# Rows of attention reordered by dimension and head, and another order of attention's steps: gated attention and GLU on one core

## The chip, the cores and the metric

The kernel runs on one core of one Trainium2 chip. The metric is the device time of one execution in microseconds (us). The core has five engines that run their own instruction streams side by side and wait for each other by semaphores: TensorE (PE, matrix products), VectorE (DVE), ScalarE (ACT), GpSimd (POOL) and SyncE (SP). DMAs are issued here from SP's queue, a few from ACT's, and an instruction stream is in order: what stands behind a waiting instruction waits too.

## The reference, cut to what matters

The input is x of 2048 rows by 576. One half is linear attention with 32 heads of 18 dimensions, the other a gated MLP of width 4608, and a gate g per row mixes them.

```python
qkv = (x @ wqkv) as (3, H=32, S, Dh=18); q, k, v = qkv
phi = lambda t: where(t > 0, t + 1, exp(t)) + 1e-6
pq, pk = phi(q), phi(k)
kv = einsum("bhsd,bhse->bhde", pk, v);  z = sum over s of pk
o  = einsum(pq, kv) / (einsum(pq, z) + 1e-6)
a  = o.reshape(S, D) @ wo
b  = (gelu(x @ w_gate) * (x @ w_up)) @ w_down
g  = sigmoid((x * gate_w).sum(-1))
out = g * a + (1 - g) * b
```

## The kernel before, in words

All products are done on TensorE as several products of rounded high and low parts, so that float32 precision is kept. The MLP is a block algorithm with seven products in place of eight. The work has four stages. The first (to about 119 us) projects the keys and sums key features against x. The second (to about 146 us) forms the states `st`, `st4` (keys by values for each head) and the key sums, and begins the queries. The third, which this study is about, runs from 146 to 290 us: a list written out by hand, `PLAN` (lines 33 to 44), of 249 steps. Line 888 calls them in this order, and each step appends its instructions to the engines' streams; so the list sets the order on every engine, and an instruction runs when its operands, its buffer and the ones ahead of it on its engine let it. The fourth stage is the MLP: loops over chains of seven products (line 985) and the down projection (line 1062).

The queries come in four blocks b of 512 rows; blocks 2 and 3 come first in the list, then 0 and 1. Their features are laid over partitions in five groups g of 128, 128, 128, 128 and 64 rows (`QORDER`, line 21, gives the feature at each row). The steps, with the line of their instructions in the profile:

- q(b, g) (L467): PE, 14 products into one of three PSUM buffers `bank` (10 for g = 4). qe (L480, L481): relu and exp on ACT; qd (L485): max and add on DVE, which frees the bank. qs (L475, L476) folds the two halves of group 4, qz (L471) clears.
- so (L595 to L605) takes the states out of PSUM, multiplies them by a mask of "same head" and splits them into high and low parts. ks(g) (L611, L612) forms `zmk`, the key sums of each head as columns, on DVE.
- wl(g) loads wo (SP), ws(g) splits it (L588 ACT, L589 POOL), ho(g) multiplies it with the state (L622 PE), he(g) takes that out (L82 ACT, L83 DVE) to `kw`. ro(g) copies two rows of group 4 into group g by DMA (SP), rd (L634, L635) duplicates group 4.
- h(b, g) splits the query features (L645 ACT, L646 DVE) into one of two `hl` buffers; n(b, g) (L655 PE) multiplies them with `zmk` into `den`, the denominators.
- rc(b, half) takes `den` out (L686 ACT, L687 DVE), forms the reciprocal (L688 DVE) and stores it to DRAM (L689 SP). rl(b, half) (L694 SP) loads it back so that each partition has the reciprocal of its own head, in two DMAs: 126 rows read with the 7 heads outermost and each repeated 18 times, and 2 rows.
- sc(b, t) (L701 DVE) multiplies 128 rows by the reciprocals, sp(b, t) (L706 ACT, L707 and L708 DVE) splits them into one of two `p` buffers, m(b, t) (L717 PE) is 28 products with `kw` into one of two `pair` buffers, mo(b, t) (L724 ACT) scales them by the gate into one of two `ga` buffers and stores that to DRAM from ACT's queue (L726).
- For the MLP: tl, ts, tp load, sum (L313 to L316 DVE) and split (L668 ACT, L671 POOL) blocks of x; al, as, ao and ul, us, uo do sums ahead on POOL with loads and stores; xo(i) stores blocks of x to DRAM (L740 SP); w0 (ACT's queue) and w1 (SP's queue) (L767) load prepared weights; g (L743) loads ACT's table for gelu; f0 to f3 (L790 PE) are the first four of the seven products of the MLP's first chain; o0 to o2 close and open memory pools.

The order of tiles in a buffer ring follows the list: a new tile takes the buffer that the list has freed for the longest time.

Of the kernel before, what the change touches and what calls it, by code (L numbers as in the profile page):

```python
# [15 lines left out]
H, DH = 32, 18  # L16
# [13 lines left out]

PLAN = """
h20 wl4 q24 so q31 al3 h21 ws4 wl0 wl3 qs2 qe24 qz3 ks0 ks2 qe31 wl1 ao1 q30 qd24 ks3 ho4 qd31 ks1 n20 q32 ws0
ws1 qe30 he4 h22 as2 qe32 qd30 n21 ho1 h23 al4 ks4 wl2 ho0 he1 q33 ao2 ro1 n22 ws2 ws3 he0 h24 q34 qe33 qd33 ho2
al5 qs3 ho3 n23 he2 as4 ro2 he3 qd32 n24 qe34 o0 ro0 as3 xo0 rc20 ao4 h30 ro3 qd34 rl20 h31 rc21 qz0 as5 xo1 q00
rl21 q01 qe00 tl0 q02 n30 qe02 qd02 n31 ao3 qd00 h32 qe01 ao5 q03 n32 sc21 ul0 xo2 h33 ul1 sc20 qd01 us0 h34 q04
qe03 ul2 n33 sp20 n34 rd h00 sp21 rc30 us1 qs0 m20 sc22 m21 rc31 qd03 qe04 sp22 sc23 q11 us2 ts0 q10 tl1 rl30
h01 mo21 sp23 tp0 mo20 qz1 qd04 qe10 qe11 n00 rl31 qd11 n01 uo0 m22 h02 qd10 mo22 sc30 m23 sc31 sp30 q12 sp31
mo23 qe12 ts1 uo1 q13 n02 h03 h04 uo2 sc32 m30 tl2 n03 n04 tp1 qd12 rc00 q14 rc01 m31 h10 sc33 n10 h11 sp32 qe13  # L40
mo31 sp33 rl00 qs1 o1 mo30 qd13 n11 h12 qe14 rl01 h13 qd14 m32 mo32 w0 n12 sc00 m33 g sc01 sp00 h14 n13 sp01 n14
mo33 m00 rc10 sc03 sc02 mo00 ts2 sp02 rl10 tp2 rc11 m01 rl11 m02 sp03 o2 sc10 w1 f0 mo02 mo01 f1 m03 sc11 sp10
mo03 sp11 sc12 f2 sc13 m10 sp12 mo10 f3 m11 m12 sp13 mo11 m13 mo12 mo13
"""

SEQUENCE = (1, 6, 2, 7, 5, 4, 3)
# [6 lines left out]
def tile_gated_mix(ctx, tc, xt, xs, xn, wk, wv, wq, wo, wgu, wdn, cst, out):  # L53
    nc = tc.nc
# [15 lines left out]
    def f32(ap):  # L70
        return ap.bitcast(F32)
# [9 lines left out]
    def split(hi, lo, raw):  # L81
        nc.scalar.activation(hi, raw, AF.Copy)  # L82
        nc.vector.tensor_tensor(lo, raw, f32(hi), OP.subtract)  # L83
# [319 lines left out]
    for t in range(FIRST, NST):  # L403
# [3 lines left out]
        n, now = DO.get(t, 0), early[0] if t in MAKE else None  # L407
# [229 lines left out]
    hl_of, den_of, rb_of, p_of, m_of = {}, {}, {}, {}, {}  # L637
# [42 lines left out]
    HB = BS // 2  # L680

    def rc(b, h):
        c = slice(h * HB, (h + 1) * HB)
        rb = rb_of[b, h] = pools["q"].tile([128, NG, HB], F32, name="rb", bufs=3)
        ps, rd = den_of[b], rb[:HROWS * NG, 0]
        nc.scalar.activation(rd, ps[64:64 + HROWS * NG, c], AF.Copy, bias=EPS)  # L686
        nc.vector.tensor_tensor(rd, rd, ps[:HROWS * NG, c], OP.add)  # L687
        nc.vector.reciprocal(rd, rd)  # L688
        nc.sync.dma_start(rden_d[b, h], rd)  # L689

    def rl(b, h):
        src = rden_d[b, h]
        for k, (rows, heads, times) in enumerate(((slice(0, 126), 7, DH), (slice(126, 128), 1, 2))):
            nc.sync.dma_start(rb_of[b, h][rows], bass.AP(  # L694
                tensor=src.tensor, offset=src.offset + 7 * k * NG * HB,
                ap=[[NG * HB, heads], [0, times], [1, NG * HB]]))
# [5 lines left out]

    def sp(b, t):
        r = r_of[b][:, :, t * 128:(t + 1) * 128]
        p = p_of[b, t] = pools["q"].tile([128, 2, NG, 128], F32R, name="p")
        nc.scalar.activation(p[:, 0], r, AF.Copy)  # L706
        nc.vector.tensor_tensor(p[:, 1, :4], r[:, :4], f32(p[:, 0, :4]), OP.subtract)  # L707
        nc.vector.tensor_tensor(p[64:, 0, 4], r[:64, 4], f32(p[:64, 0, 4]), OP.subtract)  # L708

    def m(b, t):  # L710
        p = p_of.pop((b, t))
        y = m_of[b, t] = pair()
        n = 0
        for g in range(NG):
            for a, wl in ((0, 0), (0, 1), (1, 0))[:3 if g < 4 else 2]:
                for i in range(2):
                    nc.tensor.matmul(y[:, i, :288], p[:, a, g], KW[g][:, wl, i * 288:(i + 1) * 288],  # L717
                                     start=(n == 0), stop=(n == 13))
                n += 1

# [167 lines left out]
    for word in PLAN.split():  # L888
        name = word.rstrip("0123456789")
# [267 lines left out]
```

## Time and profile before

| what | before |
|---|---|
| median of 3 runs | 1503.09 us (1502.42 to 1506.62) |
| the profiled execution | 1507.52 us |
| its span, first to last instruction | 1505.7 us |
| PE, DVE, ACT, POOL busy in the span | 1490.1, 1016.9, 548.7, 717.6 us |
| PE busy in 155 to 180 us | 25.00 of 25 us |
| PE busy in 180 to 204 us | 22.64 of 24 us |
| PE busy in 204 to 245 us | 35.94 of 41 us |
| PE busy in 258 to 290 us | 29.45 of 32 us |
| mean granted PE clock in 245 to 258 us | 0.80 |

In the rows of the profile "x14" is a count of instructions. A row of a timeline has start, duration (us), engine, line, operation, tiles and shape, and in brackets how long the engine was idle before it and what ended that. A row of the chain of work has start, duration and what ran. A row of the waits has the engine and its instruction, what it waited for, us in total, how often, and the longest. A row of stretches has the length, the busy time of PE, PEld (weight loads), DVE, ACT and POOL with counts, then the granted clock of PE (1.00 is full), the busy share of the 16 DMA engines and GB/s.

### The profile page before, as it was taken

How to read it: one execution, taken by the hardware profiler on the slowest of the kernel's cores; microseconds unless marked ns; L12 is line 12 of the kernel's file. 1: busy time of each engine (PE TensorE's matmuls, PEld its weight loads, DVE VectorE, ACT ScalarE, POOL GpSimd, SP SyncE). 2: the span in 40 equal slices, each digit the busy share in tenths (PEclk: the TensorE clock that was granted, in tenths of full speed). 3: DMA queues.
4: the chain of work that ended last, by engine and by line, in shares of the span. 5: the costliest groups of instructions: out<-in, count | busy, mean ns of one | idle time of the engine just before them, and what ended most of it. 6: DMA issues, size and time to landing. Idle time of an engine off the chain costs nothing.

```text
span 1505.7 us, 21568 instructions
## 1 busy us (share of the span) xinstructions
PE 1490.1 (99%) x8312; PEld 1316.1 (87%) x8312; DVE 1016.9 (68%) x1351; ACT 548.7 (36%) x716; POOL 717.6 (48%) x516
## 2 busy tenths in 40 slices
PE   9999998999999999999999999999999999999999
PEld 9999788878888888888888888888899999999999
DVE  8887787384666556666556665557677777777775
ACT  7554654333222232222332222332244354444431
POOL 2663533155654644644645645544257364553710
PEclk9999999999999999999999999999999999999999
DMA  7563374662332223332223332224777656565564
GB/s 249 167 203 117 143 265 176 228 258 91 140 140 98 98 104 121 140 125 99 105 93 138 140 120 95 105 102 166 283 281 265 209 166 215 170 213 186 198 204 132
DMA packets 98752, 246.53 MB, mean 164 GB/s; under 512 B 9105, under 2 KB 36433, under 8 KB 96217
## 3 DMA queue, kind: packets, MB, share of 16 engines
q1 hardware_dynamic: 95768, 235.58, 45.4%
q10 hardware_dynamic: 2880, 9.57, 1.7%
q8 instruction: 65, 1.06, 0.3%
q14 instruction: 39, 0.31, 0.1%
HBM read 156.80 MB, written 88.28 MB: 163 GB/s over the span
## 4 chain that ended last, share of the span: by engine, by line
PE 96%; DVE 2%; DMA 1%; ACT 1%; issue 0%; SPq 0%; ACTq 0%; DVEq 0%
PE bank L790 54%; PE bank L1050 26%; PE bank L467 4%; PE pair L717 3%; PE pair L270 2%; PE pair L225 2%; PE kpair L270 2%; PE kpair L225 2%; DMA raw<-wk 1%; DMA ga_d<-ga 1%; PE den L655 0%; PE pair L622 0%; PE pair L518 0%; DVE rb L688 0%; ACT ga L724 0%
## 5 line engine op out<-in xcount | busy, mean ns | idle before, releaser
L790 PE MATMUL bank<-xo,wg 128*128 128x512 f32 x1764 | 414.1, 395 | 1.6 <-ACT ga L724 0.8
L790 PE MATMUL bank<-xo,wu 128*128 128x512 f32 (+1 forms) x1715 | 401.7, 394 | 0.0
L790 PEld LDWEIGHTS bank<-xo,wg 128*128 128x128 f32 x1764 | 332.2, 188 | 79.4 <-DVE e L823 1.2
L790 PEld LDWEIGHTS bank<-xo,wu 128*128 128x128 f32 (+1 forms) x1715 | 323.3, 189 | 75.4
L1058 DVE SCALAR_TENSOR_TENSOR acc<-bank,gate,acc 128x288 f32<-128x288 f32 x288 | 140.4, 512 | 69.7 <-PE bank L1050 67.5
L309 POOL TENSOR_TENSOR stage<-stage 128x384 f32<-128x384 f32 x132 | 153.2, 1181 | 49.5 <-DMA stage<-wgu 46.9
L832 ACT ACTIVATE p<-bank 128x512 f32<-128x512 f32 x72 | 43.1, 598 | 337.2 <-PE bank L790 337.2
L804 POOL TENSOR_TENSOR wg<-stage,wg 128x768 fp32r<-128x768 f32 (+1 forms) x34 | 73.2, 2153 | 179.5 <-ACT wg L803 178.1
L804 POOL TENSOR_TENSOR wu<-stage,wu 128x768 fp32r<-128x768 f32 (+1 forms) x34 | 80.1, 2356 | 148.5 <-ACT wu L803 147.2
L1050 PE MATMUL bank<-wd,xo 128*128 128x288 f32 x1008 | 135.8, 294 | 0.0
L1050 PEld LDWEIGHTS bank<-wd,xo 128*128 128x128 f32 x1008 | 134.1, 188 | 0.0
L936 POOL TENSOR_TENSOR xo<-stage,xo 128x432 fp32r<-128x432 f32 x44 | 65.1, 1501 | 115.1 <-ACT xo L934 114.0
L837 DVE TENSOR_TENSOR u<-bank,p 128x512 f32<-128x512 f32 x72 | 49.5, 687 | 90.8 <-PE bank L790 84.4
L1050 PE MATMUL bank<-xo 128*128 128x288 f32 x792 | 107.1, 295 | 0.1
L1050 PEld LDWEIGHTS bank<-xo 128*128 128x128 f32 x792 | 105.7, 188 | 0.5 <-DVE u L826 0.4
L936 POOL TENSOR_TENSOR wd<-stage,wd 128x432 fp32r<-128x432 f32 x40 | 59.5, 1515 | 89.3 <-ACT wd L934 89.3
L823 DVE TENSOR_TENSOR e<-bank,u 128x512 f32<-128x512 f32 x54 | 37.2, 691 | 76.7 <-PE bank L790 76.5
L823 DVE TENSOR_TENSOR f<-bank,u 128x512 f32<-128x512 f32 x54 | 37.3, 692 | 72.8 <-PE bank L790 72.5
L813 ACT ACTIVATE f<-f 128x512 f32<-128x512 f32 x54 | 34.1, 633 | 133.6 <-DVE f L823 133.5
L941 POOL TENSOR_TENSOR stage<-stage 128x432 f32<-128x432 f32 x48 | 75.8, 1606 | 0.0
L851 DVE TENSOR_TENSOR u<-bank,u 128x512 f32<-128x512 f32 x72 | 49.8, 692 | 35.1 <-PE bank L790 32.8
L717 PEld LDWEIGHTS pair<-kw,p 128*128 128x128 f32 x448 | 63.1, 196 | 4.1 <-ACT p L706 2.2
(198 smaller groups left out, 2321.9 us busy)
## 6 DMA issues: line engine op xcount, KB each, us to landing
h_d<-sx SPq DMA_DIRECT2D x108, 256.0 KB
stage<-wgu SPq DMA_DIRECT2D x34, 768.0 KB
xo<-h_d SPq DMA_DIRECT2D x29, 768.0 KB
e<-h_d SPq DMA_DIRECT2D x28, 768.0 KB
hraw<-h_d SPq DMA_DIRECT2D x27, 768.0 KB
h_d<-e SPq DMA_DIRECT2D x72, 256.0 KB
h_d<-f SPq DMA_DIRECT2D x72, 256.0 KB
stage<-wdn SPq DMA_DIRECT2D x6, 1728.0 KB
```

The costliest lines, as they stand in the source:

```text
L225: nc.tensor.matmul(out_t[:, :n], xa, kvw[i][:rows, r, lo:lo + n], start=(k == 0), stop=(k == 13))
L270: nc.tensor.matmul(y[:, n, :KH], a, p[:, n * KH:(n + 1) * KH], start=(k == 0), stop=(k == len(ops) - 1))
L309: nc.gpsimd.tensor_tensor(o, a, b, OP.subtract)
L467: nc.tensor.matmul(ps[:wa.shape[1]], wa, xa, start=(k == 0), stop=(k == len(ops) - 1), skip_group_check=g == 4)
L717: nc.tensor.matmul(y[:, i, :288], p[:, a, g], KW[g][:, wl, i * 288:(i + 1) * 288], start=(n == 0), stop=(n == 13))
L790: nc.tensor.matmul(ps, w_, x_, start=start and i == 0, stop=i == 6, skip_group_check=not start)
L804: nc.gpsimd.tensor_tensor(w[:, i, 3:5], src[:, :, 0:2], f32(w[:, i, 0:2]), OP.subtract)
L823: nc.vector.tensor_tensor(es[i], a, b, OP.add)
L936: nc.gpsimd.tensor_tensor(w[:, 1, c], src[:, c], f32(w[:, 0, c]), OP.subtract)
L941: nc.gpsimd.tensor_tensor(draw[:, o, c], draw[:, x, c], draw[:, y, c], OP.subtract)
L1050: nc.tensor.matmul(y, h[:, hl, g, t * 128:(t + 1) * 128], w[:, wl, g * 288:(g + 1) * 288], start=k in (1, 5) and n == 0, stop=n == len(ops ...
L1058: nc.vector.scalar_tensor_tensor(o, y, gate[:, 1, st:st + 1], o, op0=OP.mult, op1=OP.add)
```

## The change

The feature rows of groups 0 to 3 are no longer 7 heads by 18 dimensions and two rows of heads 28 to 31, but 16 dimensions by 7 heads (112 rows, dimension outermost), then the last two dimensions of each of the 7 heads (14 rows), and the same two rows as before. Group 4 interleaves likewise. The mask, the selecting columns and the weights' columns follow on the host; the mask of group 4 is one of its own. rl still has two DMAs: 112 rows with 16 repeats outermost over 7 heads, and 16 rows of 8 heads by 2. The tile p has 9 blocks of 128 columns in place of 10. And `PLAN` is the same 249 steps in another order.

```diff
-QORDER = [d for g in range(4) for d in (*range(126 * g, 126 * g + 126), 568 + 2 * g, 569 + 2 * g)] + [*range(504, 568)]
+def features(g):
+    heads = [7 * g + h for h in range(7)] if g < 4 else [31, 28, 28, 29, 29, 30, 30]
+    if g < 4:
+        return [DH * heads[p % 7] + p // 7 for p in range(112)] + [DH * n + 16 + j for n in heads for j in range(2)] + [
+            568 + 2 * g, 569 + 2 * g]
+    return [DH * heads[p % 7] + p // 7 + (9 if p % 7 in (2, 4, 6) else 0) for p in range(64)]
+
+QORDER = [d for g in range(5) for d in features(g)]
...
-CW = 126 + NG * 64
+CM = 126 + 72
+CW = CM + NG * 64
...
 PLAN = """
-h20 wl4 q24 so q31 al3 h21 ws4 wl0 wl3 qs2 qe24 qz3 ks0 ks2 qe31 wl1 ao1 q30 qd24 ks3 ho4 qd31 ks1 n20 q32 ws0
-ws1 qe30 he4 h22 as2 qe32 qd30 n21 ho1 h23 al4 ks4 wl2 ho0 he1 q33 ao2 ro1 n22 ws2 ws3 he0 h24 q34 qe33 qd33 ho2
-al5 qs3 ho3 n23 he2 as4 ro2 he3 qd32 n24 qe34 o0 ro0 as3 xo0 rc20 ao4 h30 ro3 qd34 rl20 h31 rc21 qz0 as5 xo1 q00
-rl21 q01 qe00 tl0 q02 n30 qe02 qd02 n31 ao3 qd00 h32 qe01 ao5 q03 n32 sc21 ul0 xo2 h33 ul1 sc20 qd01 us0 h34 q04
-qe03 ul2 n33 sp20 n34 rd h00 sp21 rc30 us1 qs0 m20 sc22 m21 rc31 qd03 qe04 sp22 sc23 q11 us2 ts0 q10 tl1 rl30
-h01 mo21 sp23 tp0 mo20 qz1 qd04 qe10 qe11 n00 rl31 qd11 n01 uo0 m22 h02 qd10 mo22 sc30 m23 sc31 sp30 q12 sp31
-mo23 qe12 ts1 uo1 q13 n02 h03 h04 uo2 sc32 m30 tl2 n03 n04 tp1 qd12 rc00 q14 rc01 m31 h10 sc33 n10 h11 sp32 qe13
-mo31 sp33 rl00 qs1 o1 mo30 qd13 n11 h12 qe14 rl01 h13 qd14 m32 mo32 w0 n12 sc00 m33 g sc01 sp00 h14 n13 sp01 n14
-mo33 m00 rc10 sc03 sc02 mo00 ts2 sp02 rl10 tp2 rc11 m01 rl11 m02 sp03 o2 sc10 w1 f0 mo02 mo01 f1 m03 sc11 sp10
-mo03 sp11 sc12 f2 sc13 m10 sp12 mo10 f3 m11 m12 sp13 mo11 m13 mo12 mo13
+wl4 ws4 qz3 q24 q30 so ao1 h20 q31 ks0 wl0 ho4 wl3 qs2 ws0 qe30 n20 ks2 wl1 qd30 qe24 h21 he4 al4 al3 h22 qe31
+qd31 xo0 ks4 as2 ks1 ro1 qd24 ks3 ho0 ro2 ws1 ws3 he0 q32 ho1 qe32 wl2 ws2 he1 n21 h23 q33 ho3 he3 ho2 qe33 qd32
+n22 h24 qd33 he2 ro0 ro3 o0 n23 ao2 q34 tl0 al5 qs3 n24 rc20 q01 qe34 q02 as5 qz0 qd34 as3 rl20 as4 qe01 rc21
+ao4 xo1 q00 qd01 h30 n30 h32 sc21 rl21 qe00 q03 h31 qe02 rd qd00 n31 sc20 qe03 ao3 ao5 ul0 ul1 qd02 n32 sp20 h34
+h33 us0 ul2 q04 qd03 sp21 xo2 qs0 m20 qe04 n33 ts0 sc22 n34 rc31 rc30 us1 rl31 mo20 m21 rl30 sc23 h00 sp22 q10
+tl1 sp23 q11 n00 qd04 us2 h02 m22 qz1 h01 tp0 qe11 mo22 n01 mo21 sc30 uo0 tl2 n02 qe10 m23 qd10 sc32 q12 h04
+sp30 m30 sc31 qd11 h03 qe12 sp31 ts1 n03 q14 sc33 qd12 n04 mo30 q13 sp32 uo1 h10 mo23 m31 rc00 tp1 rc01 h11 rl00
+qs1 n10 qe13 mo31 h12 qd13 qe14 uo2 sp33 o1 sc01 g rl01 n11 m32 mo32 qd14 sc00 n12 m33 h13 w0 h14 sp00 ts2 n13
+mo33 n14 sp01 sc03 rc10 m00 rl10 tp2 m01 mo00 sc02 sp02 rc11 mo01 o2 rl11 sp03 f0 sc10 sc11 f1 m02 sp10 sc12
+mo02 m03 m10 sp11 sc13 mo03 mo10 sp12 f2 m11 sp13 w1 m12 mo11 mo12 m13 mo13 f3
 """
...
-    mask, sel = cs[:, :126], cs[:, 126:]
+    mask, mask4, sel = cs[:, :126], cs[:, 126:CM], cs[:, CM:]
...
-            nc.vector.tensor_tensor(kvm[:R, g, :R], kvm[:R, g, :R], mask[:R, :R], OP.mult)
+            nc.vector.tensor_tensor(kvm[:R, g, :R], kvm[:R, g, :R], (mask if g < 4 else mask4)[:R, :R], OP.mult)
...
     def rl(b, h):
         src = rden_d[b, h]
-        for k, (rows, heads, times) in enumerate(((slice(0, 126), 7, DH), (slice(126, 128), 1, 2))):
+        for rows, ap in ((slice(0, 112), [[0, 16], [NG * HB, 7]]), (slice(112, 128), [[NG * HB, 8], [0, 2]])):
             nc.sync.dma_start(rb_of[b, h][rows], bass.AP(
-                tensor=src.tensor, offset=src.offset + 7 * k * NG * HB,
-                ap=[[NG * HB, heads], [0, times], [1, NG * HB]]))
+                tensor=src.tensor, offset=src.offset, ap=ap + [[1, NG * HB]]))
...
-        p = p_of[b, t] = pools["q"].tile([128, 2, NG, 128], F32R, name="p")
-        nc.scalar.activation(p[:, 0], r, AF.Copy)
-        nc.vector.tensor_tensor(p[:, 1, :4], r[:, :4], f32(p[:, 0, :4]), OP.subtract)
-        nc.vector.tensor_tensor(p[64:, 0, 4], r[:64, 4], f32(p[:64, 0, 4]), OP.subtract)
+        p = p_of[b, t] = pools["q"].tile([128, 9, 128], F32R, name="p")
+        nc.scalar.activation(p[:, :5], r, AF.Copy)
+        nc.vector.tensor_tensor(p[:, 5:], r[:, :4], f32(p[:, :4]), OP.subtract)
+        nc.vector.tensor_tensor(p[64:, 4], r[:64, 4], f32(p[:64, 4]), OP.subtract)
...
-                    nc.tensor.matmul(y[:, i, :288], p[:, a, g], KW[g][:, wl, i * 288:(i + 1) * 288],
+                    nc.tensor.matmul(y[:, i, :288], p[:, 5 * a + g], KW[g][:, wl, i * 288:(i + 1) * 288],
```

More of the change, by code (lines that the diff above doesn't have):

```diff
@@ L1137 @@
     head = np.arange(126) // DH
-    cst[:126, :126] = head[:, None] == head[None, :]
+    kept = np.array(QORDER) // DH
+    cst[:126, :126] = head[:, None] == kept[None, :126]
+    last = np.concatenate([kept[512:], np.full(8, 31)]) - 28
+    cst[:72, 126:CM] = head[:72, None] == last[None, :]
     for g in range(NG):
@@ L1141 @@
             n = QORDER[QO[g] + r] // DH
-            for c in (n % 7 * NG + n // 7,) if n < 31 else (3 * NG + 4, *range(7 * NG, 7 * NG + 4)):
-                cst[r, 126 + g * 64 + c] = 1.0
+            if n < 28:
+                columns = (n % 7 * NG + n // 7,)
+            elif n < 31:
+                columns = (2 * (n - 28) + 1) * NG + 4, (2 * (n - 28) + 2) * NG + 4
+            else:
+                columns = (4, *range(7 * NG, 7 * NG + 4))
+            for c in columns:
+                cst[r, CM + g * 64 + c] = 1.0
     nc = bacc.Bacc("TRN2", target_bir_lowering=False, num_devices=1, dynamic_dma_scratch_size=512)
```

## The prediction

> **What bounds the kernel now.** First the page's head: TensorE (PE) is busy for all but 15.6 us of the span.
>
> ```profile
> span 1505.7 us, 21568 instructions
> PE 1490.1 (99%) x8312; PEld 1316.1 (87%) x8312; DVE 1016.9 (68%) x1351; ACT 548.7 (36%) x716; POOL 717.6 (48%) x516
> ```
>
> The change gives PE no matmul more or fewer, so it can only move PE's idle time and the clock. Second, the waits of PE alone from 119 to 320 us, the stretch that the reordered list fills (us in total, times, longest):
>
> ```profile
> PE den L655 <- DVE hl L646: 4.6, 3, 4.2
> PE pair L717 <- ACT p L706: 1.7, 1, 1.7
> PE bank L467 <- DVE r L485: 1.1, 1, 1.1
> PE bank L790 <- ACT ga L724: 0.8, 1, 0.8
> PE pair L717 <- DVE p L707: 0.7, 1, 0.7
> ```
>
> Third, the chain of work that ended last, over the same stretch (start, us, what), says why each came about:
>
> ```profile
> 146.34 8.88 PE bank L467 x38
> 155.21 0.80 PE pair L622 x6
> 156.01 0.46 PE den L655 x2
> 156.47 3.21 PE bank L467 x14
> ...
> 179.76 0.61 ACT r L480
> ...
> 180.40 0.64 ACT r L481
> ...
> 181.06 0.70 DVE r L485
> ...
> 181.80 3.55 PE bank L467 x14
> ...
> 202.49 0.96 DVE hl L646
> ...
> 229.81 8.48 DMA ga_d<-ga
> ...
> 238.37 0.75 ACT ga L724
> ...
> 243.24 0.61 DVE hl L646
> ...
> 243.90 0.80 PE den L655
> 244.69 13.63 PE pair L717 x84
> 258.32 3.20 PE bank L790 x14
> ...
> 272.04 0.75 ACT ga L724
> ...
> 273.97 11.65 PE pair L717 x84
> ```
>
> The largest stall is n14's, 4.2 us before 243.90. Read back: mo32 on ACT waited until 238.37 for a free `ga` buffer, which the store of mo30 held for 8.48 us; behind it on ACT stand w0, g (the activation table), sp00 and h14, and n14 waits for h14. After it three m steps (84 matmuls) took 13.63 us where the same 84 took 11.65 from 273.97 on. The stretches say why: the granted clock (the figure after the POOL column) is halved.
>
> ```profile
> 240.00:245.00 5.00, 1.10 (x4) 1.01 (x5) 2.56 (x5) 4.16 (x7) 0.00 (x0) 0.83 1.03 374
> 245.00:250.00 5.00, 5.00 (x22) 5.00 (x22) 4.79 (x6) 0.11 (x1) 0.00 (x0) 0.50 0.55 219
> ```
>
> **The change, part by part.** *The two loads of rl.* Eight rl steps load 640 KB each in two DMAs, before and after.
>
> ```profile
> rb<-rden_d SPq DMA_DIRECT2D x8, 630.0 KB
> ...
> 228.44 3.08 SPq L694 DMA_DIRECT2D rb<-rden_d  x4
> ...
> 237.27 1.56 DVE L701 SCALAR_TENSOR_TENSOR r<-r,rb 128x640 f32<-128x640 f32 x2 [0.61 <-DMA rb<-rden_d]
> ```
>
> rl00 and rl01 were issued from 228.44 and sc00 still waited for them at 237.27, 8.8 us later. That wait was 0.61 us of DVE and no wait of PE, so by itself a quicker load is worth between nothing and the stalls that a late store causes. No row shows this load with another shape. Its bounds are 8.8 us as now and 3.4 us, two loads at the 374 GB/s of the first stretch above; I take 4 to 5 us, nearer the latter. It enters the sum only as cover: sc steps never wait, and stores like the one of 8.48 us meet less traffic.
>
> [...]
>
> *Features, mask, p tile.* mask4 and the wider `cst` change no instruction's count or size; p shrinks from 10 to 9 blocks by giving up one that nothing read. All the L622, L655, L717, L706 to L708 instructions keep their shapes. Cost nothing: the wider `cst` lands before 147 us as now and nothing but so and ks reads it.
>
> *The list: stalls that go.* (a) q03, 1.1 us. PSUM has three `bank` buffers, handed on in the order in which the list frees them. The old list frees q02's first (qd02 ahead of qd00), so q03 waits for the product just finished and its relu, exp and max (179.76 to 181.76). The new one frees q01's first and has q00 and n30 between. What is late next is DVE: qd01 now ends well ahead. (b) n14, 4.2 us. The new list sets g ahead of mo32, h13 ahead of w0, h14 ahead of sp00, and runs mo30 before q13, with mo23 and mo31 between it and mo32; two `ga` buffers alternate, so mo32 takes that of mo23, stored some 8 us before. Were that store late as well, ACT would stand there again, but with g already done and h13 alone between it and n13. (c) The halved clock, 13.63 − 11.65 = 2.0 us, if no stall of that length follows elsewhere. (d) m11 at 273.97, 1.7 us: sp11 stands behind mo03 on ACT, which ran only at 272.04, long after m03, so a store held its buffer. The new list has sp11 before mo03 and sp13 before mo11. (e) 0.8 us, the fourth waits row: the bank after m13 waits for mo13 (L724). In the new list f3 (7 matmuls, half of the 3.20 us at 258.32) comes after m13 and covers it. Sum: 1.1 + 4.2 + 2.0 + 1.7 + 0.8 = 9.8 us.
>
> *The list: stalls that come.* (f) n21. It needs ks1, and the new list puts ks4 and ks1 behind he4, h22 and qd31 on DVE, with ws1 and ws3 going to POOL at the same time. How ks behaves beside POOL, and the steps ahead of it:
>
> ```profile
> 152.80 0.25 DVE L611 TENSOR_SCALAR zmk<-cs,zc 128x64 fp32r<-128x64 f32 x1
> 153.09 0.28 DVE L612 SCALAR_TENSOR_TENSOR zmk<-cs,zc,zmk 128x64 fp32r<-128x64 f32 x1
> ...
> 157.84 0.63 ACT L82 ACTIVATE kw<-pair 72x576 fp32r<-72x576 f32 x1
> 158.37 0.62 ACT L645 ACTIVATE hl<-r 128x512 fp32r<-128x512 f32 x1
> ...
> 162.70 2.81 POOL L589 TENSOR_TENSOR wos<-raw,wos 128x576 fp32r<-128x576 f32 x2 [0.60 <-ACT wos L588]
> 162.84 1.36 DVE L612 SCALAR_TENSOR_TENSOR zmk<-cs,zc,zmk 64x64 fp32r<-64x64 f32 x1
> ...
> 164.22 1.34 DVE L611 TENSOR_SCALAR zmk<-cs,zc 64x64 fp32r<-64x64 f32 x1
> ```
>
> PE comes to n21 after q24, q30, q31 (8.88 us from 146.34), ho4, n20, ho0, q32 and ho1: 146.34 + 8.88 + 0.80 + 0.46 + 0.80 + 3.21 + 0.80 = 161.3 us. ACT frees ho4's result at 156.0, then he4 0.63, h22 0.62, qe31 0.61 + 0.64: 158.5, and qd31 on DVE 0.70: 159.2. There ks4 (four instructions) meets ws1 and ws3, 1.4 us each on POOL. An instruction of 0.25 us alone took 1.34 beside them, ending as theirs ended. So ks4 ends near 162.3 and ks1 (0.25 + 0.28) near 162.9: n21 waits 1.6 us. Bounds: nothing if POOL is out of the way (159.2 + 1.06 + 0.53 = 160.8), 3.8 us if all four are caught (159.2 + 4 × 1.35 + 0.53 = 165.1). Behind n21 on PE all the rest is queued.
>
> [...]
>
> (g) m01: ts2 now stands between sp00 and sp01 on DVE; one wait of the kind in the fifth waits row, 0.7 us. (h) f0 moves one m step forward and needs w0's 2240 KB.
>
> ```profile
> wg<-wp_d ACTq DMA_DIRECT2D x1, 2240.0 KB
> ...
> 239.56 0.50 ACTq L767 DMA_DIRECT2D wg<-wp_d  x1
> ```
>
> PE reaches m00 at 244.69 − 4.2 − 1.1 + 1.6 = 241.0 at the latest, 239.7 if smaller waits go too; with two m steps of 3.88 (11.65 / 3) f0 stands at about 247.5. ACT issues w0 near 237: mo32 without its 3 us wait and h13 ahead of it. That leaves 10.5 us; at 374 GB/s the load takes 6.0, and from before it is known to take at most 18.8 (239.56 to f0 at 258.32, no wait shown). I take 1.0 us of wait, near the low end since the rl loads should be out of the way; bounds 0 and 8.3. *SP's queue.* xo0 (1280 KB) moves ahead of the first ro and tl0 ahead of rl20; both leave the busy stretch of 185 to 205 us, and their issue waits for nothing. wl2 moves behind ro1 and ro2 and so behind he4 (about 157.4); ws2 and ho2 want it some 5 and 10 us later. If it took 8 us as the rl loads do, ws2 would hold ACT for about 3 us, and he1 and h23 behind it, ahead of n23. I count that at nothing, since few transfers are in flight there. w1 stands later in the list, but on SP it still follows rl11 directly.
>
> New stalls: 1.6 + 0.7 + 1.0 = 3.3 us. **Sum: 9.8 − 3.3 = 6.5 us less.** The profiled execution took 1507.5 us (span 1505.7 and 1.8 around it), the median is 1503.1 and the lowest run 1502.4. So a typical run had less of these losses. The stalls of (a), (b), (d), (e) follow from the order and I take them as in every run; the halved clock may or may not follow a stall of 4 us. With it in the median: 1503.1 − 6.5 = 1496.6; without: 1498.6. I take the middle, **1497.5 us**.
>
> **Rivals.** *DVE takes the place* (1501.5 us). From about 181 to 207 us the new order leaves DVE hardly a gap: rc31 and rc30 with their reciprocals, ts0 and five sc/sp steps precede h00, sp22 and h01, for which n00, m22 and n01 wait. I see about 1 us of room at each. If n21 waits 3 us and two of these are late by 1 to 2 us, 6.5 becomes about 2.5. For it: the chain of before still runs over DVE at 202.49. Against: PE hardly waited there then.
>
> *The loads stay slow* (1500.5 us). If rl20, issued near 177, again takes 8 us, sc21, which DVE reaches near 182, holds DVE for some 3 us ahead of h31 and n31 and PE waits nearly as long: 6.5 − 3 = 3.5. For it: no row shows the new shape. [...]
>
> *Slower: w0 is late at f0* (1516 us). Place: f0. Nearest row of a big transfer in a busy stretch:
>
> ```profile
> 187.77 1.04 SPq L740 DMA_DIRECT2D xop_d<-xo  x1
> ...
> 204.23 1.92 ACT L668 ACTIVATE xo<-xc 128x2048 fp32r<-128x2048 f32 x1 [3.99 <-DMA xop_d<-xo]
> ```
>
> 1280 KB were 16.5 us on their way there. At that rate 2240 KB take 28.9 us: 237 + 28.9 − 247.5 = 18.4 us of wait in place of 1.0, and the halved clock (2.0) again: 18.4 + 2.0 − 1.0 − 6.5 = 12.9 us slower. It turns the sign from a wait of 5.5 us on (5.5 + 2.0 = 6.5 + 1.0), a load of 16 us. Against: before's own 18.8 us bound and 374 GB/s while it ran.
>
> **How the numbers follow.** A measurement of this kernel tells about 0.3%, 4.5 us, from no change: faster is below 1498.6, slower above 1507.6. Forecast 0.63: of it 0.53 below 1498.6, 0.10 within. DVE takes the place 0.20: 0.02 faster, 0.18 within. Loads stay slow 0.08: 0.02 and 0.06. w0 late 0.09: 0.02 within, 0.07 slower. Sums: faster 0.57, same 0.36, slower 0.07. Range: low 1491.5, all of 9.8 and the small waits gone and none new (1503.1 − 11.5); high 1504, which takes in the DVE rival with its bounds and the mild end of w0 and leaves out some 0.12 above.
>
> **What would show it.** Right: no PE wait over 3 us between 119 and 320, granted clock 1.00 to its end, the end of the last m and f some 6 us earlier than 286, and n21 (den) waiting 1 to 2 us for zmk near 161. sc steps wait for no DMA, and a pair of rl loads lands within 5 us. Wrong: a wait of PE at f0 for a DMA; waits of den or pair for DVE summing to over 4 us; matmuls slower outside this stretch.

## The result, and the profile after

| | before | after |
|---|---|---|
| median (range, runs) | 1505.84 us (1501.75 to 1506.99, 8) | 1499.04 us (1495.90 to 1501.57, 8) |
| the profiled execution | 1507.52 us | 1498.99 us |
| ratio after / before, 95% interval | | 0.9962, 0.9947 to 0.9977 |

The ratio is 5.7 us (3.5 to 8.0) of 1505.84: faster, and inside the range of 1491.5 to 1504. First the head of the page of after, and PE's waits between 119 and 320 us (us in total, times, longest):

```profile
span 1497.2 us, 21559 instructions
PE 1487.6 (99%) x8312; PEld 1315.0 (88%) x8312; DVE 1015.5 (68%) x1351; ACT 548.6 (37%) x716; POOL 716.9 (48%) x516
```

```profile
PE den L666 <- DVE zmk L623: 1.7, 1, 1.7
PE bank L800 <- DVE e L833: 0.8, 1, 0.8
PE pair L727 <- ACT p L716: 0.7, 1, 0.7
PE den L666 <- DVE hl L657: 0.2, 1, 0.2
```

Lines have moved by 10 or 11: L666 is n, L727 m, L716 sp, L734 mo, L711 sc, L705 rl, L800 f. Of the waits of before, the 4.2 us of n14, the 1.7 of m11, the 1.1 of q03, the 0.8 behind mo13 and the 0.7 at L707 are gone; the 0.8 us at L833 lies in the MLP and stands in both kernels. New are n21's 1.7 us and 0.7 us of an m step. The next two fences have the stretches where the clock was halved before (the granted clock is the figure after POOL), and PE's timeline.

```profile
240.00:245.00 5.00, 5.00 (x39) 4.96 (x39) 4.80 (x9) 2.63 (x3) 0.00 (x0) 1.00 0.90 359
245.00:250.00 5.00, 5.00 (x30) 4.48 (x29) 4.13 (x5) 2.67 (x5) 4.81 (x3) 1.00 0.31 106
```

```profile
163.27 0.73 PE L666 MATMUL den<-hl,zmk 128*128 128x512 f32 x2 [1.69 <-DVE zmk L623]
...
239.21 0.50 PE L666 MATMUL den<-hl,zmk 128*128 128x512 f32 x1 [0.22 <-DVE hl L657]
239.55 7.68 PE L727 MATMUL pair<-kw,p 128*128 128x288 f32 x56
247.06 3.40 PE L800 MATMUL bank<-xo,wg 128*128 128x512 f32 x14
...
267.65 7.91 PE L727 MATMUL pair<-kw,p 128*128 128x288 f32 x56 [0.70 <-ACT p L716]
```

n14 (239.21) waits 0.22 us in place of 4.2, m00 and m01 run on at full clock (1.00), and f0 (247.06) waits for nothing. The MLP's bank that waits for L833 in both kernels starts at 304.08 in place of 313.64, so 9.6 us were won by then (6 were forecast). Working it out from the rows: waits of 8.9 us became 2.6 (6.3 us), and PE ran at half clock (0.50) from 243.9 to 250.1 before. That cost 2.4 us by the rows of the instructions: three m steps took 13.63 us in place of 11.65, and n14 0.80 from its start to m00's, in place of 0.34. By PE's busy time from 119 us to that bank, 184.9 us before and 181.6 after, it is up to 3.3 us. Together that makes 8.7 to 9.6. After that, 0.9 us goes to a wait in the down projection that before does not have (L1060 for the accumulation at L1068), so the profiled executions differ by 8.5 us, more than the medians.

So far it looks as predicted. One line doesn't: DVE's sc steps do wait for their loads (first the row of DVE's waits in after, then its timeline and SP's).

```profile
DVE r L711 <- DMA rb<-rden_d: 8.5, 4, 3.4
```

```profile
177.20 1.40 SPq L705 DMA_DIRECT2D rb<-rden_d  x2
182.53 0.83 DVE L711 SCALAR_TENSOR_TENSOR r<-r,rb 128x640 f32<-128x640 f32 x1 [0.74 <-DMA rb<-rden_d]
...
201.26 2.77 SPq L705 DMA_DIRECT2D rb<-rden_d  x4
209.68 1.60 DVE L711 SCALAR_TENSOR_TENSOR r<-r,rb 128x640 f32<-128x640 f32 x1 [2.77 <-DMA rb<-rden_d]
```

A pair took 5.3 us from issue to the step that waits, two pairs issued together 8.4. In before the same wait is 2.8 us, one old pair took 7.9 us (175.41 to 183.32), two issued together 8.2 and 8.8. So, each in its own list, a single new pair is quicker and two together hardly are. The new list asks for its loads sooner, and so it waits longer. PE paid nothing for it. Whether that is luck or need is what the experiments ask first.

### The profile page after: what moved, and what is told of

Its sections match the earlier page's. It is cut to its first block, busy times and chain, and to the rows that moved or that the text cites. A ratio compares the mean times of both kernels' runs of the same rounds, so it can differ in the third digit from the quotient of the medians.

```text
span 1497.2 us, 21559 instructions
## 1 busy us (share of the span) xinstructions
PE 1487.6 (99%) x8312; PEld 1315.0 (88%) x8312; DVE 1015.5 (68%) x1351; ACT 548.6 (37%) x716; POOL 716.9 (48%) x516
## 4 chain that ended last, share of the span: by engine, by line
PE 91%; DVE 4%; DMA 2%; ACT 1%; issue 1%; POOL 0%; SPq 0%; ACTq 0%; DVEq 0%
PE bank L800 53%; PE bank L1060 24%; PE bank L478 3%; PE pair L281 2%; PE pair L236 2%; PE kpair L236 2%; PE kpair L281 2%; PE pair L727 1%; DMA rb<-rden_d 1%; DMA ga_d<-ga 1%; DMA stage<-wdn 1%; POOL wd L946 0%; DMA xo<-h_d 0%; DVE e L826 0%; DVE r L711 0%
## 5 line engine op out<-in xcount | busy, mean ns | idle before, releaser
L800 PE MATMUL bank<-xo,wg 128*128 128x512 f32 x1764 | 414.0, 395 | 0.8 <-DVE e L833 0.8
L800 PE MATMUL bank<-xo,wu 128*128 128x512 f32 (+1 forms) x1715 | 401.5, 394 | 0.0
L800 PEld LDWEIGHTS bank<-xo,wg 128*128 128x128 f32 x1764 | 332.2, 189 | 78.7 <-DVE e L833 1.2
L800 PEld LDWEIGHTS bank<-xo,wu 128*128 128x128 f32 (+1 forms) x1715 | 323.3, 189 | 75.1
L1068 DVE SCALAR_TENSOR_TENSOR acc<-bank,gate,acc 128x288 f32<-128x288 f32 x288 | 140.0, 511 | 69.2 <-PE bank L1060 66.6
L1060 PE MATMUL bank<-wd,xo 128*128 128x288 f32 x1008 | 135.8, 294 | 0.0
L1060 PEld LDWEIGHTS bank<-wd,xo 128*128 128x128 f32 x1008 | 134.1, 188 | 0.0
L1060 PE MATMUL bank<-xo 128*128 128x288 f32 x792 | 107.1, 295 | 0.1
L1060 PEld LDWEIGHTS bank<-xo 128*128 128x128 f32 x792 | 105.7, 188 | 0.5 <-DVE u L836 0.4
L833 DVE TENSOR_TENSOR f<-bank,u 128x512 f32<-128x512 f32 x54 | 37.3, 692 | 72.8 <-PE bank L800 72.4
L833 DVE TENSOR_TENSOR e<-bank,u 128x512 f32<-128x512 f32 x54 | 37.2, 691 | 70.9 <-PE bank L800 70.8
L823 ACT ACTIVATE e<-e 128x512 f32<-128x512 f32 x54 | 34.0, 632 | 89.4 <-DVE e L833 89.4
```

The source lines that it names most:

```text
L800: nc.tensor.matmul(ps, w_, x_, start=start and i == 0, stop=i == 6, skip_group_check=not start)
L823: nc.scalar.activation(es[i], es[i], AF.Gelu_apprx_tanh)
L833: nc.vector.tensor_tensor(es[i], a, b, OP.add)
L1060: nc.tensor.matmul(y, h[:, hl, g, t * 128:(t + 1) * 128], w[:, wl, g * 288:(g + 1) * 288], start=k in (1, 5) and n == 0, stop=n == len(ops ...
L1068: nc.vector.scalar_tensor_tensor(o, y, gate[:, 1, st:st + 1], o, op0=OP.mult, op1=OP.add)
```

## The experiments

Theory at the outset: the order of the list made the gain, the loads' shape was cover. Rival: one needs the other.

| kernel | median, us | ratio to before, 95% interval |
|---|---|---|
| layout_alone | 1505.76 | 0.9991 (0.9980 to 1.0002) |
| list_alone | 1512.39 | 1.0037 (1.0025 to 1.0050) |
| by_sevens | 1518.62 | 1.0073 (1.0060 to 1.0085) |
| old_g_early | 1500.44 | 0.9956 (0.9941 to 0.9971) |
| layout_g_early | 1500.57 | 0.9953 (0.9940 to 0.9965) |
| after_g_late | 1500.14 | 0.9951 (0.9938 to 0.9965) |
| ks1_first | 1497.03 | 0.9941 (0.9927 to 0.9956) |
| sp12_first | 1497.96 | 0.9940 (0.9927 to 0.9952) |
| w1_late | 1497.21 | 0.9933 (0.9921 to 0.9945) |
| gap_and_w1 | 1495.90 | 0.9930 (0.9916 to 0.9943) |
| sc_behind | 1497.36 | 0.9931 (0.9919 to 0.9944) |

The ratio is to runs of before on the same chip (medians 1507.0 to 1507.75 us there), 5 runs of each and 11 of layout_alone. load_alone is no kernel of this kind and has no ratio. Differences of 1 to 2 us between the versions of after (from ks1_first on) are within these intervals and are read from the traces; a part of their lead over after is the clock, which was granted at 0.998 or 0.999 on the mean in four of the eight runs of after (1498.1 to 1501.6 us) and in one of five of ks1_first and of sp12_first. How little such a lead tells is seen in sp12_first, which lies 1.1 us below after by the medians though PE waits 0.5 us longer in its trace (3.9 us in 119 to 320 in place of 3.4).

**The change in two halves.** layout_alone is after with the old list (the diff), list_alone is before with the new list (the same rows the other way round):

```diff
 PLAN = """
-wl4 ws4 qz3 q24 q30 so ao1 h20 q31 ks0 wl0 ho4 wl3 qs2 ws0 qe30 n20 ks2 wl1 qd30 qe24 h21 he4 al4 al3 h22 qe31
+h20 wl4 q24 so q31 al3 h21 ws4 wl0 wl3 qs2 qe24 qz3 ks0 ks2 qe31 wl1 ao1 q30 qd24 ks3 ho4 qd31 ks1 n20 q32 ws0
...
```

> The new feature rows with the old list. Theory (the order of the list does nearly all, the loads' shape is cover at most): within 1.5 us of the kernel before, its stalls in 119 to 320 us as before: q03 some 1.1 us, n14 about 4 us behind mo32 waiting for the store of ga, m11 1.7 us, the bank after m13 0.8 us. Rival (the quicker load clears the way for stores): the wait of mo32 for its store shrinks below 5 us, n14's stall falls below 2 us, and the time falls by 3 to 6 us.

The theory held: no sc step waits for a load any more, and PE's stalls stay but for the 0.7 us at L707 (den 5.1 us, pair 1.8, bank 1.1 and 0.8); the store ahead of mo32 still took 7.5 us. In the old list the quicker load is worth nothing that can be measured.

> The new list with the old feature rows and the old two loads (126 rows with 7 heads outermost, and 2 rows). Theory (order does it): within 1 us of the kernel after, some 5 to 6 us below before; sc steps on DVE wait for their loads in total 3 to 10 us more than the 8.5 us of after, and PE hardly waits for it. Rival (the load's shape is needed by the new order): sc21 and sc01 hold DVE long enough that h31, sp or qd come late and PE waits 2 us or more for DVE between 180 and 260 us, so that the time is 3 us or more above after.

The theory fell, and so did the prediction's step. PE's waits in 119 to 320 us:

```profile
PE pair L717 <- ACT p L706: 4.1, 3, 2.8
PE pair L717 <- DVE p L707: 2.6, 2, 1.4
PE den L655 <- DVE hl L646: 2.3, 3, 1.6
PE pair L717 <- ACT ga L724: 1.7, 1, 1.7
PE den L655 <- DVE zmk L612: 1.7, 1, 1.7
PE bank L790 <- DVE e L823: 0.8, 1, 0.8
PE bank L467 <- DVE r L485: 0.5, 1, 0.5
```

These are 13.7 us, against 3.4 in after. DVE's waits and the timelines of SP and DVE in list_alone name the cause:

```profile
DVE r L701 <- DMA rb<-rden_d: 26.5, 6, 8.2
```

```profile
203.97 3.07 SPq L694 DMA_DIRECT2D rb<-rden_d  x4
...
216.55 0.83 DVE L701 SCALAR_TENSOR_TENSOR r<-r,rb 128x640 f32<-128x640 f32 x1 [8.19 <-DMA rb<-rden_d]
...
236.12 1.43 SPq L694 DMA_DIRECT2D rb<-rden_d  x2
...
253.03 1.24 DVE L701 SCALAR_TENSOR_TENSOR r<-r,rb 128x640 f32<-128x640 f32 x1 [3.16 <-DMA rb<-rden_d]
```

The two pairs that took 8.4 us in after take 12.6 here, and the one beside w0's 2240 KB takes 16.9. DVE stands at sc30 for 8.2 us, sp30 and m30 behind it. So the new list alone is slower than before by 0.37%, and the new layout with its loads, worth nothing in the old list, is worth some 11 us in the new one (1.0037 − 0.9962).

**Is it the number of DMA engines?** load_alone has the two loads of each shape by themselves:

```diff
+OLD = (((0, 126), [[ROW, 7], [0, 18]], 0), ((126, 128), [[ROW, 1], [0, 2]], 7))
+NEW = (((0, 112), [[0, 16], [ROW, 7]], 0), ((112, 128), [[ROW, 8], [0, 2]], 0))
...
+    def old_126():
+        load(OLD[0]); nc.vector.tensor_scalar(seen, into, 1.0, None, op0=mybir.AluOpType.mult)
...
+    def new_112():
+        load(NEW[0]); nc.vector.tensor_scalar(seen, into, 1.0, None, op0=mybir.AluOpType.mult)
```

> Leaves out the whole computation: only the two loads of rl, read from x, each pair followed by a DVE instruction that waits for it; four turns of old pair, new pair, and each of the four loads by itself, then four turns of each pair with a load of 2240 KB issued from ACT's queue just before. Theory (the old load runs on a part of the DMA engines, the new one on all): old pair 5 to 8 us from issue to the waiting instruction, new pair 3.5 to 4.5 us; the 2-row load costs little by itself; beside the 2240 KB the old pair takes 10 us or more and the new one 5 to 7. Rival (it is the traffic, not the shape): both pairs within 1 us of each other when alone, and equally late beside the big load.

The stretches of 1 us in which one load ran alone (the last two figures are the busy share of the 16 DMA engines and GB/s): the old pair, the new pair, the 126 rows, the 112 rows.

```profile
43.00:44.00 1.00, 0.00 (x0) 0.00 (x0) 1.00 0.46 189
...
49.00:50.00 1.00, 0.00 (x0) 0.00 (x0) 1.00 0.99 369
...
56.00:57.00 1.00, 0.00 (x0) 0.00 (x0) 1.00 0.46 189
...
62.00:63.00 1.00, 0.00 (x0) 0.00 (x0) 1.00 1.10 399
```

The old load kept 0.46 of the engines' time busy at 189 GB/s, close to the 0.44 that 7 of 16 would give (an estimate of how many worked, since the rows don't number the engines); the new one kept all of it busy (0.99 and 1.10 by the rows) at 369 and 399 GB/s, twice the rate. Yet by itself the new one saves little; DVE's wait for four loads of 126 rows (L30) and of 112 rows (L39):

```profile
L30 DVE TENSOR_SCALAR seen<-into 128x1280 f32<-128x1280 f32 x4 | 3.3, 828 | 24.6 <-DMA into<-x 24.6
L39 DVE TENSOR_SCALAR seen<-into 128x1280 f32<-128x1280 f32 x4 | 3.3, 828 | 18.4 <-DMA into<-x 18.4
```

That is 6.15 and 4.6 us a load. The third turn's old and new pair, in DVE's timeline:

```profile
78.64 0.83 DVE L27 TENSOR_SCALAR seen<-into 128x1280 f32<-128x1280 f32 x1 [6.48 <-DMA into<-x]
84.14 0.83 DVE L36 TENSOR_SCALAR seen<-into 128x1280 f32<-128x1280 f32 x1 [4.67 <-DMA into<-x]
```

So alone a pair gains 1.8 us, half of its moving time: at the rates of the rows 640 KB take some 3.5 us (189 GB/s) and 1.8 us (369 GB/s), an estimate, and the other 3.0 and 2.9 us of the two waits stay. The turns beside 2240 KB did not show the 10 us or more against 5 to 7 that were expected: the first new pair that met a large load took 9.0 us from the end of the instruction that freed its buffer, the first old pair 8.9. They decide nothing, since the buffer of the small load came free ahead of the large one's (by 0.9 us in that new pair's turn and by 2.0 in the old one's), so that the two shapes did not meet the same traffic.

by_sevens puts outermost counts of 7 back into after (and one of 2, for the last 14 of the 112 rows), with nothing else of the old layout:

```diff
-        for rows, ap in ((slice(0, 112), [[0, 16], [NG * HB, 7]]), (slice(112, 128), [[NG * HB, 8], [0, 2]])):
+        for rows, ap in ((slice(0, 49), [[0, 7], [NG * HB, 7]]), (slice(49, 98), [[0, 7], [NG * HB, 7]]),
+                         (slice(98, 112), [[0, 2], [NG * HB, 7]]), (slice(112, 128), [[NG * HB, 8], [0, 2]])):
```

> The kernel after with the load of 112 rows cut into 49, 49 and 14 rows, so that the outermost counts are 7, 7 and 2 as in the old load, with the same bytes; the layout of the features and the list stay those of after. By load_alone a load of 7 outermost keeps 7 of the 16 DMA engines busy (0.44 to 0.46 of them at 184 to 189 GB/s). Theory (the new list needs the loads on all engines; nothing else of the layout matters): sc steps wait for their loads as in list_alone, 20 us or more in total, PE waits 8 us or more between 119 and 320 us, and the time is 8 to 14 us above after. Rival (what made list_alone slow is another part of the old layout, or the pieces go to different engines): within 3 us of after.

The direction is the theory's, the size beyond it: by the ratios 17 us above after. sc waited 33.0 us, PE 16.4 in 119 to 320, and its clock was halved three times (to 0.50 from 220 us, 0.55 from 266 and 0.50 from 286). The stretches of by_sevens and then of after behind the same step, rl31 and rl30:

```profile
208.00:209.00 1.00, 1.00 (x10) 1.00 (x9) 0.97 (x2) 0.97 (x2) 0.43 (x1) 1.00 0.47 184
209.00:210.00 1.00, 1.00 (x8) 0.96 (x7) 0.10 (x1) 0.85 (x2) 1.00 (x1) 1.00 0.44 179
210.00:211.00 1.00, 1.00 (x6) 0.62 (x6) 0.00 (x0) 0.59 (x2) 1.00 (x2) 1.00 0.47 174
...
222.00:224.00 2.00, 1.48 (x6) 1.48 (x7) 1.94 (x4) 0.46 (x2) 0.00 (x0) 0.50 1.08 404
```

```profile
209.00:210.00 1.00, 1.00 (x10) 1.00 (x9) 0.32 (x1) 0.66 (x1) 1.00 (x2) 1.00 0.89 352
210.00:211.00 1.00, 1.00 (x10) 1.00 (x9) 1.00 (x1) 0.90 (x2) 1.00 (x2) 1.00 0.96 382
```

The four pieces of rl31 had been issued by then, and still no more than 0.47 of the engines' time was busy until 211, as much as one load of 7 outermost had kept busy by itself (0.46): the pieces together moved no faster than that one, at 174 to 184 GB/s against 189. Whether they shared the same engines is not shown. by_sevens also issues four DMAs for each rl (3.1 us of SP in place of 1.4), and its count of 2 is one that the old load did not have; either may be why it is slower than list_alone. That was not told apart.

**What made the gain, then?** old_g_early is before with one row of the list changed:

```diff
-mo31 sp33 rl00 qs1 o1 mo30 qd13 n11 h12 qe14 rl01 h13 qd14 m32 mo32 w0 n12 sc00 m33 g sc01 sp00 h14 n13 sp01 n14
+mo31 sp33 rl00 qs1 o1 mo30 qd13 n11 h12 qe14 rl01 h13 qd14 g m32 mo32 n12 sc00 m33 sc01 h14 w0 sp00 n13 sp01 n14
```

> The kernel before with one row of its list changed: g ahead of mo32, and h14 ahead of w0 and sp00 on ACT; mo32 still waits for the store of mo30. Theory (n14's 4.2 us come from what stands on ACT between the late mo32 and h14, and the halved clock follows that stall): n14 waits 1 to 2.5 us, the clock stays at 1.00 in 240 to 260 us, the time is 3 to 5 us below before. Rival (the store alone sets it): n13 or n14 waits as long, since h14 still stands behind mo32; the time is within 1 us of before, and the clock is halved again.

It gained 6.6 us (0.9956; the interval is 4.4 to 8.9), as much as the whole change, from three moved names (g, h14, w0), which were not tried one by one. The theory said 3 to 5. In its timelines mo32 still waits for the store, but only 1.22 us, since g stands in that gap, and n14 0.79 us. The clock stays full (1.00). A third stall went too, which the theory did not foresee: m11's 1.7 us, although sp11 still stands behind mo03. The stores of mo02 and mo01 now left at 255.66 and 256.80 us, and mo03 found its buffer free; in before they left at 261.28 and 262.43, behind w1's load (260.26).

```profile
237.59 0.74 ACT L724 ACTIVATE ga<-pair,gate 128x576 f32<-128x576 f32 x1 [1.22 <-DMA ga_d<-ga]
...
240.20 0.50 PE L655 MATMUL den<-hl,zmk 128*128 128x512 f32 x1 [0.79 <-DVE hl L646]
```

```profile
240.00:245.00 5.00, 4.80 (x35) 4.76 (x36) 4.80 (x8) 2.32 (x5) 0.00 (x0) 1.00 1.05 366
```

> old_g_early with the new feature rows and loads. Theory (in the old list the stalls follow from the order, and the loads have time enough): within 1 us of old_g_early, some 6 to 7.5 us below before. Rival (the quick loads bring the store of mo30 in earlier too): 1.5 us or more below old_g_early.

The same within the interval: with the old list put right the layout is still worth nothing. The other way round, after_g_late takes g's place from after:

```diff
-qs1 n10 qe13 mo31 h12 qd13 qe14 uo2 sp33 o1 sc01 g rl01 n11 m32 mo32 qd14 sc00 n12 m33 h13 w0 h14 sp00 ts2 n13
+qs1 n10 qe13 mo31 h12 qd13 qe14 uo2 sp33 o1 sc01 rl01 n11 m32 mo32 w0 qd14 sc00 n12 m33 g h13 sp00 h14 ts2 n13
```

> The kernel after with w0, g, sp00 and h14 of its last rows put back into the old order among themselves (w0 behind mo32, g behind m33, h13 behind g, h14 behind sp00). Theory (of the two parts of step (b), the freed ga buffer of mo32 and the place of g, the store wait is what cost, and after avoids that since mo30 runs before q13): mo32 does not wait, n13 or n14 waits below 2 us, no halved clock, and the time is 0 to 2 us above after. Rival (the place of g is what counts): n13 and n14 wait 3 us or more in total and the halved clock is back, 4 us or more above after.

As the theory had it: mo32 waited 1.08 us for m32 and for no store, n14 1.03 us, the clock stayed full (1.00 in every stretch from 180 to 300 us), and the time is that of after. Of the two parts of step (b) either one is enough.

**The stalls that are left in after.** First n21's. DVE's rows in after, then POOL's:

```profile
159.27 1.50 DVE L622 TENSOR_SCALAR zmk<-cs,zc 64x64 fp32r<-64x64 f32 x1
160.80 1.37 DVE L623 SCALAR_TENSOR_TENSOR zmk<-cs,zc,zmk 64x64 fp32r<-64x64 f32 x1
162.19 0.25 DVE L622 TENSOR_SCALAR zmk<-cs,zc 64x64 fp32r<-64x64 f32 x1
```

```profile
159.28 2.81 POOL L600 TENSOR_TENSOR wos<-raw,wos 128x576 fp32r<-128x576 f32 x2 [2.55 <-ACT wos L599]
```

Two of ks4's instructions took 1.50 and 1.37 us beside two of POOL's, and the other two, of the same shapes, 0.25 and 0.27 once POOL was done.

```diff
-qd31 xo0 ks4 as2 ks1 ro1 qd24 ks3 ho0 ro2 ws1 ws3 he0 q32 ho1 qe32 wl2 ws2 he1 n21 h23 q33 ho3 he3 ho2 qe33 qd32
+qd31 xo0 ks1 as2 ks4 ro1 qd24 ks3 ho0 ro2 ws1 ws3 he0 q32 ho1 qe32 wl2 ws2 he1 n21 h23 q33 ho3 he3 ho2 qe33 qd32
```

> The kernel after with ks1 and ks4 swapped on DVE. Theory (n21's 1.7 us wait comes from ks1 standing behind ks4, whose instructions wait for POOL's ws1 and ws3): ks1 runs before ws1 begins or is caught for one pair at most, n21's wait falls to 0 to 0.3 us, and the time is 1.0 to 1.7 us below after. [...]

The theory held in part: ks1's own first pair is caught (1.50 and 1.37 us from 159.14), the rest of ks4 no longer stands ahead of n21, which waits 0.64 us in place of 1.7.

Then the 0.70 us at 267.65 in after. ACT's timeline:

```profile
256.19 0.35 ACTq L736 DMA_DIRECT2D ga_d<-ga  x1
...
265.44 0.74 ACT L734 ACTIVATE ga<-pair,gate 128x576 f32<-128x576 f32 x1 [6.12 <-DMA ga_d<-ga]
```

mo10 waits for mo02's store, 9.2 us on its way, with sp12 behind it (at 266.86) and m12 behind that.

```diff
-mo02 m03 m10 sp11 sc13 mo03 mo10 sp12 f2 m11 sp13 w1 m12 mo11 mo12 m13 mo13 f3
+mo02 m03 m10 sp11 sc13 mo03 sp12 mo10 f2 m11 sp13 w1 m12 mo11 mo12 m13 mo13 f3
```

> The kernel after with sp12 ahead of mo10 on ACT. Theory (m12's 0.70 us wait comes from sp12 standing behind mo10, which waits for a store that travels beside w1's load): m12 does not wait, the time is 0.7 us below after. Rival (the wait goes to the next in turn): m11 or m13 waits instead, since the pair buffer of m10 is freed later or sp12 itself waits for sc12, and the time is within 0.3 us of after.

The theory fell. m12 waited 1.41 us all the same, now for mo10 itself, which frees the `pair` buffer that m12 writes (PE's timeline):

```profile
267.69 2.51 PE L727 MATMUL pair<-kw,p 128*128 128x288 f32 x17 [1.41 <-ACT ga L734]
```

Every step behind a late store is late in turn, so the store itself is to be mended. w1's 2240 KB were issued at 256.23, beside it. w1_late issues them later, and from ACT's queue in place of SP's; the two were not told apart.

```diff
-mo02 m03 m10 sp11 sc13 mo03 mo10 sp12 f2 m11 sp13 w1 m12 mo11 mo12 m13 mo13 f3
+mo02 m03 m10 sp11 sc13 mo03 mo10 sp12 w1 f2 m11 sp13 m12 mo11 mo12 m13 mo13 f3
...
-        (nc.sync if i else nc.scalar).dma_start(f32(W[i]), wp_d[i])
+        nc.scalar.dma_start(f32(W[i]), wp_d[i])
```

> The kernel after with w1's load of 2240 KB issued from ACT's queue behind mo10 and sp12, in place of SP's queue behind the last rl. Theory (mo02's store took 9.2 us since w1 was issued beside it): that store lands within 6 us, mo10 does not wait, m12's stall of 0.70 us is gone, sc12's wait of 3.4 us for the last rl falls below 1 us, and the time is 0.7 us below after, if the second chain of the MLP does not wait for w1. Rival (the store is slow for itself, or the last rl loads hold it): mo10 waits as before, and w1, later, makes the second chain's first product wait.

With w1 6 us later, mo02's store was back before mo10 asked for the buffer at 261.05 (issued at 255.52, so it took at most 5.5 us), and m10 to m12 run as one:

```profile
262.44 11.35 PE L727 MATMUL pair<-kw,p 128*128 128x288 f32 x84
```

sc12 still waited 2.8 us for its load where less than 1 was expected.

> w1_late with ks1 ahead of he4 on DVE, where DVE was idle for 0.86 us before 157.00. Theory: ks1 ends well before ws1 begins on POOL near 159.3, n21 does not wait, so 1.7 us less than w1_late and 2.4 us less than after, about 1496.5 us. Rival (the pair ho0, he1 or q32 is the next in turn at n21): n21 or its neighbour waits for ACT or a bank instead, and the gain over w1_late is below 0.7 us.

```diff
-wl4 ws4 qz3 q24 q30 so ao1 h20 q31 ks0 wl0 ho4 wl3 qs2 ws0 qe30 n20 ks2 wl1 qd30 qe24 h21 he4 al4 al3 h22 qe31
+wl4 ws4 qz3 q24 q30 so ao1 h20 q31 ks0 wl0 ho4 wl3 qs2 ws0 qe30 n20 ks2 wl1 qd30 qe24 h21 ks1 he4 al4 al3 h22 qe31
-qd31 xo0 ks4 as2 ks1 ro1 qd24 ks3 ho0 ro2 ws1 ws3 he0 q32 ho1 qe32 wl2 ws2 he1 n21 h23 q33 ho3 he3 ho2 qe33 qd32
+qd31 xo0 ks4 as2 ro1 qd24 ks3 ho0 ro2 ws1 ws3 he0 q32 ho1 qe32 wl2 ws2 he1 n21 h23 q33 ho3 he3 ho2 qe33 qd32
```

n21 no longer waits, ks1 ran at 155.99 and PE went on:

```profile
161.35 0.64 PE L666 MATMUL den<-hl,zmk 128*128 128x512 f32 x2
```

But 1.27 and 0.21 us of wait came at n13 and n14, since PE was now ahead of rl00's load: sc01 held DVE for 2.67 us, with qd14, h13 and h14 behind it. Of the 1.7 us, 1.3 are seen in the medians, less than the intervals tell. It has the lowest median of all, some 3 us below after, and the intervals of the two to before are clear of each other. But they were not run side by side, and the trace accounts for 0.5 us of it (2.9 us of PE's waits in 119 to 320 in place of 3.4), so the size of its lead over after is not shown.

> gap_and_w1 with sc01 and sc00 behind qd14, h13 and h14 on DVE. In gap_and_w1, sc01 stood on DVE for 2.67 us waiting for rl00's load, with qd14, h13 and h14 behind it, and n13 and n14 waited 1.5 us. Theory: n13 and n14 do not wait, m00 waits for sp00 0.5 us or less, the time is 0.5 to 1.5 us below gap_and_w1. Rival (the wait moves to m00, which needs sc00 and so the same load): m00 waits 1 to 1.5 us, the time is within 0.4 us.

```diff
-qs1 n10 qe13 mo31 h12 qd13 qe14 uo2 sp33 o1 sc01 g rl01 n11 m32 mo32 qd14 sc00 n12 m33 h13 w0 h14 sp00 ts2 n13
+qs1 n10 qe13 mo31 h12 qd13 qe14 uo2 sp33 o1 g rl01 n11 m32 mo32 qd14 h13 w0 n12 m33 h14 sc00 sp00 sc01 ts2 n13
```

The rival had the time right: the ratio is that of gap_and_w1. n13 and n14 don't wait, m00 waits 0.38 us for sp00 and m01 0.57 for sp01. But its reason, the same load, is not what the chain of work shows (start, us, what):

```profile
236.24 0.84 DVE r L711
...
241.10 0.70 DVE xc L326
...
243.18 3.39 PE pair L727 x24
```

sc00 (236.24) waits for no load; it runs straight behind h13 and h14, and sp01's low parts stand behind ts2's sums (L324 to L327). The order on DVE sets the time here, at the place that the prediction had named as (g).

## Why the prediction was right, and where it was not

- **Base.** The forecast was 5.6 us below 1503.1, a median of three runs. The ratio gives 5.7 us below 1505.84, so the difference was right; the base was 2.7 us higher, the medians are 6.8 us apart, and so 1497.5 became 1499.04. That the difference fits to 0.1 us is in part luck. The parts were summed to 6.5 us for the profiled execution and came to 8.5 there, and the 5.6 came from counting the 2.0 us of the halved clock as half.
- **(a), (b), (d), (e)**: their stalls of 1.1, 4.2, 1.7 and 0.8 us are gone, of n14's 0.2 is left. **(d)** does not follow from the order of sp11 and mo03 alone, as the prediction took it: old_g_early keeps that order and loses the stall. Its kind came back at m12 with 0.7 us: a store beside w1, which the prediction did not follow. **(c)** was sized at 2.0 from m steps alone; with n14 it is 2.4, and up to 3.3 by PE's busy time.
- **(f)** was 1.69 us for 1.6, at 163.27 for 161.3 plus 1.6, and for the reason given: ks1_first and gap_and_w1 remove it in two steps. Two of ks4's instructions took 1.50 and 1.37 us in place of 0.25 and 0.27, beside instructions of 1.4 us on POOL; by what means POOL holds them up is not shown. **(g)** and **(h)** cost nothing: m00 and m01 run as one from 239.55, and w0 needed at most 11.4 us (235.70 to 247.06). The rival "DVE takes the place" did not come: n00, m22 and n01 don't wait.
- **The step that failed** is the first: "It enters the sum only as cover: sc steps never wait". The 4 to 5 us that were forecast for two rl loads were the author's estimate between two bounds, and no run had shown the new shape; two took 8.4 us, and even one alone 5.3 to 6.5, so that sc waited four times. The total came out right since PE was spared. But list_alone shows that the cover is worth some 11 us (by_sevens, with twice as many DMAs, 17): without it the list is slower than before. The rival "The loads stay slow" had the right mechanism and was priced at 3 us for one place, sc21. In list_alone sc21 did wait 3.7 us, and PE 0.9 behind it, but sc steps waited at five more places. The prediction gave it 1500.5 us; its measured size is 1512.4.
- The prediction put 6.2 of its 9.8 us on n14 and the clock behind it, and the rest on other moves. old_g_early shows that one row of the list carries as much as the whole change, m11's 1.7 us with it. What the rest of the new order adds, and then takes by n21, m12 and earlier demands on the loads, is below what the runs tell apart.

## What to carry to other kernels

Price each half of a change in the surroundings that the other half makes: a quicker load is worth nothing where it has slack and 11 us where the order has used the slack up. For an in-order engine, look first for what stands between a late instruction and the one that the bottleneck needs; moving a table load and two of its neighbours was as good here as a new order of everything. And when a wait is moved past its victim and the stall stays, as in sp12_first, look at the transfer: in w1_late it was enough to move what travels beside it.

## What was not expected of the hardware

- The pair of loads whose large part kept 0.46 of the DMA engines' time busy is only 1.8 us slower when alone (6.48 us of wait against 4.67), but in the new list the gap widens: 12.6 against 8.4 us for two pairs. The list counts as much as the shape: in the old one two such pairs took 8.2 and 8.8 us. More moved beside them in the new one: some 2.4 MB from 204.5 to 216 us in list_alone, against 1.6 MB in the 8.2 us of before, two pairs being 1.3 of each. One such pair beside w0's 2240 KB took 16.9 us; no run has the new shape there.
- The granted clock fell to 0.50 after stalls of PE of 4.2 us (before) and 2.7 us (by_sevens, row at 222 above), but after list_alone's 2.77 us at 281.40 it stayed at 1.00, and in list_alone it fell after 1.63 and 0.21 us at 244.36:

```profile
246.00:248.00 2.00, 2.00 (x11) 2.00 (x10) 1.90 (x4) 0.62 (x2) 0.00 (x0) 0.51 0.98 303
```

Stalls of 1.8 us together were enough once and 2.77 were not, so the length of a stall alone does not decide. What else does is left open.
